# Second MLP: the square moves from layer one's outputs to layer two's loads, and the stretch of kept order moves with it

## The chip, the cores and the metric

One core of one Trainium2 chip runs the whole program. The metric is the time of the device in microseconds, the median of three runs. Smaller is better.

## The reference

Attention with a decay, then two MLPs over 2304 tokens of 512 features, each with a hidden layer of 2048. All in float32.

```python
scores = scale * q @ k.T + decay          # causal; softmax; times v -> x [2304, 512]
h = x @ w_in;   x = (h - tanh(h)) @ w_out            # first MLP
h = x @ w2_in;  r = maximum(h, 0); out = (r * r) @ w2_out   # second MLP
```

## The kernel before

**Arithmetic.** Matmuls take fp32r operands. Each float32 operand is split into a high part (a ScalarE copy into fp32r) and a low part (a VectorE subtraction), and a product is three matmuls, `PASSES`: high x high, high x low, low x high. "Split" below is always this pair, hi on ScalarE and lo on VectorE.

**Stages.** Attention first, with the first MLP threaded into it. The first MLP goes over blocks of 256 tokens, and its last block (`LAST`, 512 tokens) has 16 steps of 24 matmuls of 512 columns. In a step, `h1_atoms` makes 128 hidden features (L1010), then Tanh (L1020) on ScalarE, the difference (L1023) on VectorE, and the split (L1027, L1031) that the products of `y1_atoms` (L1050) of the next step read.

The second MLP uses a Strassen-like scheme: seven products of quarter blocks in place of eight, with sums of operands made beforehand and sums of results afterwards. In layer one, `l1_product` (L1220) computes for unit `u` (3 groups of tokens x 8 pairs of hidden chunks, 7 products of 384 columns each) products into shared PSUM banks. `after1` copies PSUM out on ScalarE (L1238), adds on VectorE (L1231), takes relu on ScalarE (L1234), and squares: on GpSimd in `store1` (L1265), or for one product in four on VectorE (L1261), which reads PSUM a second time. `put` stores the squares to `gscr` in DRAM.

In layer two there are 36 tiles `n` (9 blocks of 256 tokens x 4 chunks of the hidden features), each 42 matmuls of 256 columns (`l2_product`, L1382). For tile `n`, `g_load` brings four raw pieces by four DMAs on SP, `g_sums` makes four sums on VectorE with three instructions (L1334, L1335, L1337), and `g_split` splits seven operands of 256 (L1347 on ScalarE, 1792 elements a partition; L1348 on VectorE). `layer2` calls the sums and the split of tile `n + 2` and the load of tile `n + 4` while it issues tile `n`. There are four buffers for raw pieces and three for split ones. `after2` adds the results (L1395) and `store2` stores them. For the first tiles the same is called from layer one's list `events`, whose numbers count products: loads at 138, 145, 165, 170, sums at 146, 154, 171, and two special splits at 159 to 167.

**Weights.** The weights of the second MLP are loaded raw, decoded from their bits (`decode_w`: ScalarE L203 and L204, VectorE L210 and L212), combined to sums on GpSimd (`combine`, L256), and split piece by piece in `split_all` (L312, L313): first the two pieces of sums, then two raw pieces, `lag` calls apart. One decode at a time is under way; `decoded` starts the next. Weights of layer two go through `wscr` in DRAM and come back (`final_load`) to be split in `final_split`.

**Inputs of the second MLP.** `first_y_load` (step 6 of the last block) loads the first group, `y_sums` (step 8) makes four sums on GpSimd (L1176), and `y_split` splits seven pieces, one a step from step 9 on (L1164 on ScalarE, L1165 on VectorE).

**What sets the order.** Code is traced in the order of a clock (`cw`): each matmul atom is a tick, and `cw.later(k, fn)` traces `fn` k ticks on. The compiler's scheduler then orders each engine's instructions by its own estimate of when they are ready; every engine runs its list in that order. `pin` overrules it: while the list `ordered` isn't empty, the instruction is put behind whatever was traced last on its engine (`tc.keep_in_program_order`). `move` is a pinned DMA on SP. An instruction without `pin` can still move. Before, `ordered` is filled at unit 1 of layer one and stays filled to the end.

```python
def pin(ins):                       # L146
    if ordered:
        tc.keep_in_program_order(ins)
def store1(g, dst):                 # L1264
    nc.gpsimd.tensor_tensor(g, in0=g, in1=g, op=ALU.mult)
    cw.later(2, lambda: put(g, dst))
if n and x == 1 and n + 2 < NG:     # L1442, in layer2: x counts the products of tile n
    g_sums(n + 2)
if x == 3 and n + 2 < NG:
    g_split(n + 2)
    if n + 4 < NG:
        g_load(n + 4)
```

## Time and profile before

| | us |
|---|---|
| median of 3 runs | 1044.77 (1040.63 to 1045.24) |
| profiled execution | 1042.61 |
| its span | 1040.9 |
| TensorE busy | 1003.6 |
| VectorE, ScalarE, GpSimd busy | 721.4, 598.3, 412.1 |
| mean granted clock of TensorE, as a share of full speed | 0.986 |

In the rows below PE is TensorE, PEld its weight load, DVE VectorE, ACT ScalarE, POOL GpSimd, SP SyncE, whose queue (SPq) issues the DMAs. L12 is line 12 of the kernel. "a<-b" are the tiles written and read; a time in brackets is how long the engine sat idle before, and what released it. Matmul times are from issue to end and overlap, so the rate of matmuls is read from their count in a stretch. PEclk is the granted clock, 1.00 for 2.4 GHz and 0.50 for 1.2 GHz.

### The profile page before, as it was taken

To read this page: it belongs to the slowest core of one execution; us is meant where nothing else is said; L and a number is where in the kernel's file an instruction comes from. 1 tells how busy PE (TensorE), PEld (TensorE's weight loads), DVE (VectorE), ACT (ScalarE), POOL (GpSimd) and SP (SyncE) were. 2 spreads that over 40 slices of the span, in tenths; PEclk is the share of its full clock that TensorE was granted. 3 is DMA by queue.
4 is the path that set the end of the run, shared out by engine and by line. 5 is a ranking of instruction groups with operands and counts; after the bars stand their busy time and mean duration, and the time that the engine had idled before them with its cause. 6 is when DMAs were issued, how large, how long until landed. Compare 5 with 4: busy or idle time off the path is not lost. (4 is left out here: it accounts for less than half of the span.)

```text
span 1040.9 us, 20353 instructions
## 1 busy us (share of the span) xinstructions
PE 1003.6 (96%) x7134; PEld 953.5 (92%) x7134; DVE 721.4 (69%) x1521; ACT 598.3 (57%) x1245; POOL 412.1 (40%) x587
## 2 busy tenths in 40 slices
PE   7989999999999999999998999999999999999998
PEld 5778889999999999999997887999999898999998
DVE  4895963577677776777756578566566678777776
ACT  5895964566666666666644466557577564233332
POOL 3673542445554555544513234385756320000000
PEclk9998999999999999999998999999999999999999
DMA  8936653342343432442221232657868964344441
GB/s 233 284 109 216 207 149 74 81 121 72 90 125 95 102 105 77 122 110 67 65 66 41 95 122 81 206 204 250 269 232 263 330 203 128 102 132 133 122 122 41
DMA packets 188261, 146.97 MB, mean 141 GB/s; under 512 B 86688, under 2 KB 165856, under 8 KB 188160
## 3 DMA queue, kind: packets, MB, share of 16 engines
q1 hardware_dynamic: 188112, 145.65, 46.5%
q8 instruction: 56, 0.92, 0.4%
q14 instruction: 45, 0.37, 0.1%
q10 hardware_dynamic: 48, 0.03, 0.0%
HBM read 101.00 MB, written 39.92 MB: 135 GB/s over the span
## 5 line engine op out<-in xcount | busy, mean ns | idle before, releaser
L1050 PE MATMUL y<-ghl,w 128*128 128x256 f32 (+1 forms) x1536 | 246.7, 304 | 6.2 <-ACT ghl L1027 4.5
L1050 PEld LDWEIGHTS y<-ghl,w 128*128 128x128 f32 x1536 | 213.2, 193 | 19.5 <-ACT ghl L1027 4.9
L1010 PE MATMUL h<-x,w 128*128 128x256 f32 x1344 | 198.6, 289 | 6.4 <-POOL w L228 5.1
L1010 PEld LDWEIGHTS h<-x,w 128*128 128x128 f32 x1344 | 175.4, 191 | 11.3 <-POOL w L228 6.6
L1382 PE MATMUL o<-ws,gc 128*128 128x256 f32 x864 | 118.4, 283 | 0.0
L1347 ACT ACTIVATE gc<-graw 128x1792 fp32r<-128x1792 f32 x34 | 57.8, 1701 | 93.6 <-DVE graw L1337 52.4
L1220 PE MATMUL r<-yt,ws 128*128 128x384 f32 x576 | 107.0, 336 | 4.0 <-ACT g L1238 3.7
L1382 PEld LDWEIGHTS o<-ws,gc 128*128 128x128 f32 x864 | 110.1, 192 | 0.0
L1220 PEld LDWEIGHTS r<-yt,ws 128*128 128x128 f32 x576 | 99.9, 188 | 6.8 <-ACT g L1238 5.6
L1382 PE MATMUL o<-wq,gc 128*128 128x256 f32 x648 | 98.5, 287 | 6.2 <-DVE gc L1348 5.1
L1382 PEld LDWEIGHTS o<-wq,gc 128*128 128x128 f32 x648 | 85.8, 191 | 10.7 <-DVE gc L1348 9.3
L1265 POOL TENSOR_TENSOR g<-g 128x384 f32<-128x384 f32 x71 | 66.5, 945 | 71.2 <-ACT g L1234 52.4
L1348 DVE TENSOR_TENSOR gc<-graw,gc 128x1792 fp32r<-128x1792 f32 x34 | 68.8, 2024 | 35.3 <-ACT gc L1347 35.2
L680 ACT ACTIVATE Pb<-Pb,st 128x384 f32<-128x384 f32 (+2 forms) x80 | 55.3, 691 | 65.7 <-DVE st L671 65.4
L671 DVE CUSTOM_DVE_ANT_0 Pb<-s,Pb 128x128 f32<-128x128 f32 (+4 forms) x144 | 67.0, 481 | 29.1 <-PE s L743 23.2
L696 POOL TENSOR_SCALAR Pb<-Pb,st 128x384 f32<-128x384 f32 (+2 forms) x80 | 55.1, 689 | 77.2 <-DVE st L690 62.2
L1220 PE MATMUL r<-yt,wq 128*128 128x384 f32 x432 | 82.0, 340 | 1.4 <-DVE g L1261 1.4
L1220 PEld LDWEIGHTS r<-yt,wq 128*128 128x128 f32 x432 | 76.6, 191 | 2.8 <-DVE g L1261 2.3
L1023 DVE TENSOR_TENSOR g<-h,g 128x512 f32<-128x512 f32 x72 | 49.5, 688 | 29.1 <-ACT g L1020 27.7
L1231 DVE TENSOR_TENSOR g<-r,g 128x384 f32<-128x384 f32 x71 | 39.0, 552 | 32.2 <-ACT g L1238 17.4
L1234 ACT ACTIVATE g<-g 128x384 f32<-128x384 f32 x71 | 36.9, 522 | 42.2 <-DVE g L1231 41.8
L1020 ACT ACTIVATE g<-h 128x512 f32<-128x512 f32 x72 | 42.5, 590 | 31.4 <-PE h L1010 25.2
(169 smaller groups left out, 1929.8 us busy)
## 6 DMA issues: line engine op xcount, KB each, us to landing
graw<-gscr SPq DMA_DIRECT2D x144, 128.0 KB, 2.6
gscr<-g SPq DMA_DIRECT2D x95, 192.0 KB, 3.3
wraw<-in_moe_w_in_dram SPq DMA_DIRECT2D x32, 512.0 KB, 4.5
wraw<-in_moe_w_out_dram SPq DMA_DIRECT2D x32, 512.0 KB, 5.5
neg<-cscr SPq DMA_DIRECT2D x32, 288.0 KB, 3.3
qk<-in_k_dram SPq DMA_DIRECT2D x48, 128.0 KB, 2.8
v<-in_v_dram SPq DMA_DIRECT2D x48, 128.0 KB, 2.7
K<-K SPq DMA_DIRECT2D x32, 144.0 KB, 2.4
```

The lines of the kernel that those rows point to most:

```text
L671: nc.vector.tensor_tensor_reduce(out=d, in0=t[:rows, src : src + m], in1=d, scale=-0.125, scalar=3.0e38 if j == 0 else stat(0, x)[:rows], ...
L680: nc.scalar.activation(d, d, AF.Exp, bias=stat(len(parts) - 1, x)[:rows], scale=-1.0, accum_out=stat(2, x)[:rows])
L696: nc.gpsimd.tensor_scalar(d, d, r, 1.0, op0=ALU.mult, op1=ALU.mult)
L1010: nc.tensor.matmul(o, lhsT=win(fc, wh, dc), rhs=xpart(j, dc, xh), start=dc == 0 and wh + xh == 0, stop=dc == ND - 1 and wh == 1)
L1020: nc.scalar.activation(g, t, AF.Tanh)
L1023: nc.vector.tensor_tensor(g, t, g, op=ALU.subtract)
L1050: nc.tensor.matmul(o, lhsT=wout(fc, wh, i * P, P), rhs=ghl[:, xh, fj * n : fj * n + n], start=s == 0 and fj == 0 and wh + xh == 0 and i % ...
L1220: nc.tensor.matmul(t, lhsT=wprod(1, p, k, wh)[:, dc * P : (dc + 1) * P], rhs=yt[i, k][:, xh, dc], start=k in FRESH and dc == 0 and wh + xh ...
L1265: nc.gpsimd.tensor_tensor(g, in0=g, in1=g, op=ALU.mult)
L1347: pin(nc.scalar.activation(hi, t[:, 1:8], AF.Copy))
L1348: pin(nc.vector.tensor_tensor(lo, in0=t[:, 1:8], in1=hi.bitcast(F32), op=ALU.subtract))
L1382: nc.tensor.matmul(o, lhsT=gc[n][gh, e][:, GWHERE[k]] if n == 1 else gc[n][gh][:, GWHERE[k], e], rhs=wprod(2, 2 * q + e, k, wh), start=q = ...
```

## The change

The outputs of layer one are stored after relu, without the square: `store1` and VectorE's L1261 go, and all four results of a unit are stored two ticks after their relu. Layer two squares a tile's four raw pieces in one ScalarE instruction (128x1024) at the head of `g_sums`; the pieces and sums change places in the tile, so that the raw pieces lie side by side, and `GWHERE` follows. The three sums keep their shapes.

`ordered` is filled at step 0 of the first MLP's last block and emptied at tile 4 of layer two. Tanh, the difference and the split of the first MLP and the splits of the first group of inputs (`y_split` with `i == 0`) are pinned now, as far as `ordered` holds. In `split_all` the raw pieces of a weight come before the sums, and the delays become 1, 2 and 1 ticks.

```diff
--- before.py
+++ after.py
@@ -271,7 +271,7 @@
         v = full.rearrange("p (c f) -> p c f", c=ND)
         s4 = sums.rearrange("p (k f) -> p k f", k=4)
         work = split_plan(1, p, (v[:, :, 0:P], v[:, 2:4, P : 2 * P]), [s4[:, 0:2], s4[:, 2:4]])
-        split_all(1, p, work, 1)
+        split_all(1, p, work[2:] + work[:2], (1, 2, 1))
 
     wscr = [dram.tile([P, 7, 256], F32, name=f"wscr_{p}") for p in range(NP2)]
 
@@ -314,7 +314,7 @@
             if phase == 2:
                 pin(low)
             if x + 1 < len(work):
-                cw.later(lag, lambda: one(x + 1))
+                cw.later(lag[x], lambda: one(x + 1))
             else:
                 ready_w.add((phase, p))
                 if phase == 1:
@@ -346,7 +346,7 @@
 
     def final_split(p):
         *s_, r = stagew.pop(p)
-        split_all(2, p, split_plan(2, p, (r[:, 1:3], r[:, 0:1]), s_), 1)
+        split_all(2, p, split_plan(2, p, (r[:, 1:3], r[:, 0:1]), s_), (1, 1, 1))
 
     WHERE = {1: {5: 0, 6: 1, 7: 2, 3: 3, 1: 4, 2: 5, 4: 6}, 2: {5: 0, 6: 1, 7: 2, 4: 3, 2: 4, 3: 5, 1: 6}}
 
@@ -1017,18 +1017,18 @@
             g = m1.tile([P, 512], F32, tag="g", name=f"g1_{j}_{s}", bufs=3)
             ghl = m1.tile([P, 2, 512], F32R, tag="ghl", name=f"ghl1_{j}_{s}", bufs=2)
             gt[j, s] = ghl
-            nc.scalar.activation(g, t, AF.Tanh)
+            pin(nc.scalar.activation(g, t, AF.Tanh))
 
             def sub():
-                nc.vector.tensor_tensor(g, t, g, op=ALU.subtract)
+                pin(nc.vector.tensor_tensor(g, t, g, op=ALU.subtract))
                 cw.later(LAG['hi'], hi)
 
             def hi():
-                nc.scalar.activation(ghl[:, 0], g, AF.Copy)
+                pin(nc.scalar.activation(ghl[:, 0], g, AF.Copy))
                 cw.later(LAG['lo'], lo)
 
             def lo():
-                nc.vector.tensor_tensor(ghl[:, 1], g, ghl[:, 0].bitcast(F32), op=ALU.subtract)
+                pin(nc.vector.tensor_tensor(ghl[:, 1], g, ghl[:, 0].bitcast(F32), op=ALU.subtract))
             cw.later(LAG['sub'], sub)
 
         return [(6 * n, lambda i=i: a(i)) for i in range(len(todo))]
@@ -1070,6 +1070,8 @@
         raw = {}
         for i, (j, s) in enumerate(steps):
             last = j == LAST
+            if last and s == 0:
+                yield 0, (lambda: ordered.append(True)), j
             if s == 6 and j == LAST - 1:
                 yield 0, (lambda: raw.__setitem__(LAST, x_last())), j
             if s == 7 and j < LAST - 1:
@@ -1161,8 +1163,8 @@
 
     def y_split(i, k, src):
         t = y_tile(i, k)
-        nc.scalar.activation(t[:, 0], src, AF.Copy)
-        nc.vector.tensor_tensor(t[:, 1], src, t[:, 0].bitcast(F32), op=ALU.subtract)
+        (pin if i == 0 else lambda ins: ins)(nc.scalar.activation(t[:, 0], src, AF.Copy))
+        (pin if i == 0 else lambda ins: ins)(nc.vector.tensor_tensor(t[:, 1], src, t[:, 0].bitcast(F32), op=ALU.subtract))
 
     def y_load(i, raws_):
 
@@ -1240,7 +1242,7 @@
         def finish(g, b, r, c):
             add(g, b, g)
             relu(g, g)
-            cw.later(1, lambda: store1(g, gscr[i][:, 2 * p + r, c]))
+            cw.later(2, lambda: put(g, gscr[i][:, 2 * p + r, c]))
 
         if k == 1:
             hold(m1.tile([P, NU1], F32, tag="x", name=f"g00_{u}", bufs=4))
@@ -1258,12 +1260,7 @@
         elif k == 4:
             g = m1.tile([P, NU1], F32, tag="x", name=f"g10_{u}", bufs=4)
             relu(g, t)
-            nc.vector.scalar_tensor_tensor(g, in0=t, scalar=0.0, in1=g, op0=ALU.max, op1=ALU.mult)
-            cw.later(1, lambda: put(g, gscr[i][:, 2 * p + 1, 0]))
-
-    def store1(g, dst):
-        nc.gpsimd.tensor_tensor(g, in0=g, in1=g, op=ALU.mult)
-        cw.later(2, lambda: put(g, dst))
+            cw.later(2, lambda: put(g, gscr[i][:, 2 * p + 1, 0]))
 
     def put(g, dst):
         move(dst, g.rearrange("p (b n) -> p b n", b=3))
@@ -1273,8 +1270,6 @@
         for s in range(n):
             if s == 0:
                 load_w(2, 0)
-            if s == 1:
-                ordered.append(True)
             if s < NP2:
                 feed.upto(NF + s + 1)
             for pos, (d, k) in enumerate(STEP):
@@ -1308,7 +1303,7 @@
             events.setdefault(at, []).append((fn, arg))
     AT2 = {1: (0, 0), 6: (0, 256), 7: (1, 0), 2: (1, 256), 5: (2, 0), 4: (2, 256), 3: (3, 0)}
     ORDER2 = (1, 6, 7, 2, 5, 4, 3)
-    GWHERE = {7: 0, 5: 1, 6: 2, 3: 3, 1: 4, 2: 5, 4: 6}
+    GWHERE = {7: 3, 5: 4, 6: 5, 3: 6, 1: 0, 2: 1, 4: 2}
     graws, gc, r2 = {}, {}, {}
     NG = NBLK * 4
 
@@ -1323,18 +1318,21 @@
     def g_load(n):
         j, q = divmod(n, 4)
         t = graws[n] if n in graws else g_tile(n)
-        for slot, h, i in ((0, 1, 0), (5, 0, 0), (7, 1, 1), (6, 0, 1)):
+        for slot, h, i in ((0, 1, 0), (1, 0, 0), (3, 1, 1), (2, 0, 1)):
             src = gscr[j // 3][:, 4 * q : 4 * q + 4, h, j % 3].rearrange("p (e i) t -> p i e t", i=2)
             move(t[:, slot], src[:, i])
 
     def g_sums(n):
         t = graws[n]
-        x = t[:, 7]
-        both = bass.AP(tensor=x.tensor, offset=x.offset, ap=[x.ap[0], [0, 2], [1, 2 * P]])
-        pin(nc.vector.tensor_tensor(t[:, 1], in0=t[:, 0], in1=t[:, 5], op=ALU.subtract))
-        pin(nc.vector.tensor_tensor(t[:, 2:4].rearrange("p k e t -> p k (e t)"),
-                                    in0=t[:, 0:2].rearrange("p k e t -> p k (e t)"), in1=both, op=ALU.add))
-        pin(nc.vector.tensor_tensor(t[:, 4], in0=t[:, 6], in1=t[:, 3], op=ALU.subtract))
+        raw = t[:, 0:4].rearrange("p k e t -> p (k e t)")
+        pin(nc.scalar.activation(raw, raw, AF.Square))
+
+        def two(x, step):
+            return bass.AP(tensor=x.tensor, offset=x.offset, ap=[x.ap[0], [step * 2 * P, 2], [1, 2 * P]])
+
+        pin(nc.vector.tensor_tensor(t[:, 4], in0=t[:, 0], in1=t[:, 1], op=ALU.subtract))
+        pin(nc.vector.tensor_tensor(two(t[:, 5], 1), in0=two(t[:, 0], 4), in1=two(t[:, 3], 0), op=ALU.add))
+        pin(nc.vector.tensor_tensor(t[:, 7], in0=t[:, 2], in1=t[:, 6], op=ALU.subtract))
 
     def gc_tile(n):
         t = box2["m3"].tile([P, 2, 7, 2, P], F32R, tag=f"gc{n % 3}", name=f"gc_{n}", bufs=1)
@@ -1433,6 +1431,8 @@
     def layer2():
         third()
         for n in range(NG):
+            if n == 4:
+                ordered.clear()
             for x, k in enumerate(ORDER2):
                 if n == 0 and x < 3:
                     continue
```

## Rows read from the trace of the kernel before

**Rows 1.** the page's first part: busy time, share of the span and instructions of each engine.
```profile
PE 1003.6 (96%) x7134; PEld 953.5 (92%) x7134; DVE 721.4 (69%) x1521; ACT 598.3 (57%) x1245; POOL 412.1 (40%) x587
```

**Rows 2.** busy time by stretch: length, busy us (instructions) by engine, PEclk, DMA share, GB/s.
```profile
575.00:650.00 75.00, 73.59 (x324) 60.33 (x323) 54.09 (x80) 44.59 (x81) 24.92 (x28) 1.00 0.29 99
...
850.00:875.00 25.00, 22.37 (x178) 21.35 (x177) 22.14 (x30) 12.20 (x12) 0.26 (x1) 1.00 0.56 172
875.00:900.00 25.00, 25.00 (x210) 25.00 (x210) 17.81 (x27) 8.27 (x6) 0.00 (x0) 1.00 0.47 133
900.00:1025.00 125.00, 121.54 (x979) 118.21 (x978) 94.13 (x135) 42.83 (x30) 0.00 (x0) 1.00 0.40 116
```

**Rows 3.** TensorE's waits, 560 to 1041 us: total, times, longest.
```profile
PE y L1050 <- ACT ghl L1027: 4.5, 1, 4.5
PE r L1220 <- ACT g L1238: 3.7, 4, 2.1
...
PE r L1220 <- DVE g L1261: 1.4, 3, 0.8
...
PE o L1382 <- DVE gc L1348: 5.1, 10, 0.8
```

**Rows 4.** timeline, 545 to 580 us: start, length, instruction, [idle before <-releaser].
```profile
550.14 9.46 DVE L1165 TENSOR_TENSOR yt<-yr,yt 128x768 fp32r<-128x768 f32 x4 [1.67 <-ACT yt L1164]
...
559.52 0.68 DVE L1023 TENSOR_TENSOR g<-h,g 128x512 f32<-128x512 f32 x1
...
560.91 0.58 PE L1050 MATMUL y<-ghl,w 128*128 128x256 f32 x1 [4.48 <-ACT ghl L1027]
```

**Rows 5.** busy time by stretch, behind the two longest waits (columns as in 2).
```profile
560.90:565.20 4.30, 4.06 (x17) 3.77 (x18) 3.02 (x5) 2.17 (x3) 0.00 (x0) 0.50 0.01 4
...
824.60:828.00 3.40, 3.20 (x10) 3.20 (x11) 2.20 (x5) 1.77 (x4) 0.83 (x1) 0.50 0.92 315
```

**Rows 6.** timeline, 790 to 862 us.
```profile
819.76 1.06 ACT L312 ACTIVATE ws<-wst 128x1024 fp32r<-128x1024 f32 x1 [3.29 <-DMA wst<-wscr]
...
823.27 1.33 PE L1220 MATMUL r<-yt,ws 128*128 128x384 f32 x6 [2.13 <-ACT g L1238]
```

**Rows 7.** groups, 850 to 1041 us: shapes xcount | busy, mean ns | idle before <-releasers.
```profile
L1348 DVE TENSOR_TENSOR gc<-graw,gc 128x1792 fp32r<-128x1792 f32 x34 | 68.8, 2024 | 35.3 <-ACT gc L1347 35.2
L1347 ACT ACTIVATE gc<-graw 128x1792 fp32r<-128x1792 f32 x34 | 57.8, 1701 | 93.6 <-DVE graw L1337 52.4 <-issue 27.1 <-DMA graw<-gscr 11.6
```

**Rows 8.** timeline of VectorE, 848 to 1041 us.
```profile
914.17 0.42 DVE L1334 TENSOR_TENSOR graw<-graw 128x256 f32<-128x256 f32 x1
...
919.61 0.42 DVE L1334 TENSOR_TENSOR graw<-graw 128x256 f32<-128x256 f32 x1
...
955.64 0.69 DVE L1335 TENSOR_TENSOR graw<-graw 128x512 f32<-128x512 f32 x1
956.25 2.02 DVE L1348 TENSOR_TENSOR gc<-graw,gc 128x1792 fp32r<-128x1792 f32 x1
```

**Rows 9.** groups of the input splits (L1164 whole span, L1165 655 to 850 us).
```profile
L1164 ACT ACTIVATE yt<-yr 128x768 fp32r<-128x768 f32 x19 | 15.9, 842 | 8.5 <-POOL yr L1176 3.3 <-PE r L1220 2.3 <-DMA yr<-yscr 1.5
...
L1165 DVE TENSOR_TENSOR yt<-yr,yt 128x768 fp32r<-128x768 f32 x12 | 12.9, 1079 | 3.1 <-ACT yt L1164 3.0
```

**Rows 10.** timeline, 622 to 634 us.
```profile
630.91 2.79 PE L1050 MATMUL y<-ghl,w 128*128 128x512 f32 x11 [1.41 <-DVE ghl L1031]
```

**Rows 11.** groups, and SP's waits, both 655 to 850 us.
```profile
L1265 POOL TENSOR_TENSOR g<-g 128x384 f32<-128x384 f32 x71 | 66.5, 945 | 71.2 <-ACT g L1234 52.4 <-DVE wfull L212 7.5 <-issue 6.1
...
L1261 DVE SCALAR_TENSOR_TENSOR g<-r,g 128x384 f32<-128x384 f32 x24 | 13.2, 551 | 10.6 <-ACT g L1234 10.6
...
SPq L151 <- POOL g L1265: 65.2, 34, 8.7
```

**Rows 12.** groups of ScalarE, whole span.
```profile
L312 ACT ACTIVATE ws<-wst 128x1024 fp32r<-128x1024 f32 x5 | 5.3, 1056 | 3.5 <-DMA wst<-wscr 3.5
...
L428 ACT ACT_TABLE_LOAD x1 | 1.3, 1283 | 0.0
```


## The prediction

> **What bounds the kernel now.** The page's first part comes first: TensorE is busy for 96% of the span [rows 1]. So only what still stops TensorE, or slows it, can be gained, and the question is where the missing microseconds lie. The busy time by stage tells that. From 875 to 900 us, in the second MLP's layer two, TensorE issued 210 matmuls of 256 columns without a gap, 119 ns each; from 900 to 1025 us it issued 979, which at 119 ns are 116.5 us, so 8.5 us of these 125 were lost; from 850 to 875 us it issued 178, or 21.2 us, so 3.8 were lost [rows 2]. TensorE's own waits name the rest: one wait of 4.5 us in the first MLP's last part, 3.7 us for ScalarE's copies out of PSUM (L1238) and 1.4 us for VectorE's L1261 in layer one, 5.1 us for VectorE's L1348 in layer two [rows 3]. Three places, three mechanisms.
>
> *First MLP, at its last block.* The timeline [rows 4] shows four of VectorE's L1165 (splits of the second MLP's input, traced much later) in one stretch from 550.14 that lasts 9.46 us, because each needs a sum that GpSimd has just begun. L1023, which the running block needs, stands behind them until 559.52, and TensorE waits 4.48 us. In the 4.3 us after that, the granted clock is 0.50, the level of 1.2 GHz instead of 2.4 [rows 5]: half of 4.3, 2.15 us more. Together 6.6 us.
>
> *Layer one.* ScalarE sat 3.29 us at L312 until a DMA of staged weights landed, its copies came late, and TensorE waited 2.13 us [rows 6]; then 3.4 us ran at a clock of 0.50 [rows 5], 1.7 us more: 3.8 us.
>
> *Layer two.* VectorE goes round a closed chain: sums, then a wait for ScalarE's split (L1347, 1.70 us), then its own split (L1348, 2.02 us), then the next sums. From the sums at 914.17 to those at 919.61 that is 5.44 us [rows 7, 8], while a tile's 42 matmuls take 42 x 0.119 = 5.0 us. VectorE isn't full: 94.1 us of work in 23.3 tiles (979/42), 4.0 us each [rows 2]. Its order makes the period. Where the order was broken once, L1348 started at 956.25 straight behind the next tile's sums, with no wait in its row [rows 8].
>
> **The change, part by part.** The sum stands against the profiled execution, 1042.6 us (span 1040.9), 2.2 us under the median of the runs.
>
> *Order kept from the last block on.* Tanh, both splits behind it, the input splits, their loads on SP and the decoding of weights now stay in traced order, so the L1165 that blocked at 550 us can't stand there. Gain: 6.6 at most, nothing at least (if L1023 finds another blocker). I take 6.6, since every instruction that stood ahead of L1023 is one that is moved.
>
> What is moved has to go somewhere. Seven ScalarE splits of 0.84 us (5.9) and seven of VectorE of 1.08 (7.6) [rows 9], traced one a step, now fall into steps 9 to 15 of the block. A step is 24 matmuls; 324 took 75 us, so 5.56 us a step, 39 us for seven. VectorE was busy 54.1 of 75 us there, 72%, and gets 19% more: 91%. ScalarE goes from 59% to 75% [rows 2]. Behind a late VectorE stand L1023 and L1031, and TensorE behind these; one such wait is already there, 1.41 us [rows 10]. Bounds: nothing, or one such wait in each of the seven steps, 9.9 us. I take two, 2.8 us, as 91% leaves room on the mean but not at each moment. The twelve input loads on SP now start at step 6 and GpSimd's four sums at step 8; DMA was busy 0.29 and GpSimd 33% [rows 2], and ScalarE's next use of them is at steps 9 to 15: I cost them at nothing. Without that cover, ScalarE would stop at a pinned split with Tanh queued behind it.
>
> *Raw weights split before their sums, with delays 1, 2, 1.* No work is added; a decode ends about one atom later (5.56/6, 0.9 us), and GpSimd gets that time for the sums. Cost nothing, hidden by the steps between a decode and its first product; without them 0.9 us at layer one's start.
>
> *Layer one without squares.* 71 of GpSimd's L1265 (945 ns) and 24 of VectorE's L1261 (551 ns) go [rows 11]. GpSimd's time is off TensorE's path, VectorE's isn't: the 1.4 us of waits [rows 3] go, since PSUM is free once ScalarE's relu has read it. The stores waited 65.2 us on SP for the squares [rows 11]; now they go sooner, and the loads of weights queued behind them too. Whether that brings forward the load behind the 3.8 us is open: that load can be late from traffic alone. Between nothing and 3.8, I take the middle, 1.9.
>
> *Squares in layer two.* One on ScalarE for each of 36 tiles, 128x1024. No row shows a Square; the nearest is a ScalarE copy of the same shape, 1.056 us [rows 12]. ScalarE had 42.8 us of work in 23.3 tiles, 1.84 each [rows 2]; 2.9 of 5.0 fits beside the rest. If Square needs a table not loaded, one load is 1.283 us [rows 12]; below nothing there is none, as no work goes. Three squares fall in layer one's tail ahead of copies that TensorE needs: nothing to 3 x 1.06 us; I take 0.5, since a copy has about two products of slack.
>
> *Order freed from tile 4 on.* The next sums can run while ScalarE splits, and VectorE's 4.0 us fit into 5.0. Bounds: nothing (the compiler keeps the same order) and 8.5 us, of which I take 7, a little being left to stores and adds that now move as well. The 3.8 us before 875 us stay: those tiles keep their order. SP's loads are freed too; they are ahead by four buffers.
>
> Sum: 6.6 - 2.8 + 1.4 + 1.9 - 0.5 + 7.0 = 13.6 us; 1042.6 - 13.6 = **1029**.
>
> **Rivals.**
> *A, the last block gives its gain back.* VectorE at 91% makes a wait in each step: 9.9 instead of 2.8 us, 1036. For it: the block already shows one such wait while VectorE was less busy. Against it: the ordered layer one has only waits of this size, few of them.
> *B, freeing changes no order.* No 7 us: 1036. Against it: the one place where the order did break.
> *C, nothing new comes, and what is left goes too:* 6.6 + 1.4 + 3.8 + 8.5, 20.3 us, 1022; with the 1.41 us and part of the 3.8 before 875 us, down to 1018.
> *D, slower: the square enters the chain.* If a tile's data land only when VectorE's split of the tile before has ended, ScalarE's square, and all ScalarE work behind it, waits: the period is 5.44 + 1.06 = 6.5 us against 125/23.3 = 5.4 now, 1.1 us in each of 32 tiles, 36 us; less the 6.6 of the last block, 1072. It decides from the point where the loads run less than a tile ahead. Against it: loads wait on buffers freed four tiles earlier.
> The Trainium skill (ScalarE: Activation LUTs, Rules for kernel authors) speaks against the change here: multiplications belong on VectorE rather than ScalarE. By that rule the square would be a worse choice on ScalarE; D is how that would show, and no run here shows either. An estimate from L1348's 2.02 us for 1792 elements puts it at 1.2 us on VectorE, whose 4.0 us would become 5.2 of 5.0, so I expect the trace to go against the rule.
> *E, it doesn't do what it says:* the order in the last block binds nothing and the rest is small, 1041 to 1043.
>
> **How the numbers follow.** Forecast 42%, A 18, B 10, C 17, D 8, E 5. A measurement can tell about 0.5%, 5.2 us, from no change: faster means under 1039.5, slower over 1050. Faster: the forecast's 40, C 17, two thirds of A and B 19, and 2 of E's edge: 0.78. Slower: D, and 2 for A at twice its price: 0.10. The rest, 0.12, is the same. The range takes in C below, with 2 us for the small waits, 1016, and A, B and E above, 1042; D and the tails are left out.
>
> **What would show it.** Right: no L1165 ahead of 590 us, no TensorE gap and no 0.50 clock near 560; no wait for L1261; VectorE's sums of a tile starting before L1348 of the tile before it, and about 210 matmuls in every 25 us of layer two. Wrong: a chain period of 6 us or more there with ScalarE waiting for loads (D), an unchanged 5.4 (B), or waits of TensorE for L1027 or L1031 between 610 and 655 us that add up to over 6 us (A).

## The result, and the profile after

| | before | after |
|---|---|---|
| median of 4 runs each, us | 1043.61 (1040.63 to 1045.24) | 1027.84 (1026.06 to 1029.55) |
| ratio, 95% interval | | 0.9852 (0.982 to 0.9884) |
| profiled execution, us | 1042.61 | 1026.77 |
| its span, us | 1040.9 | 1025.1 |

The changed kernel is 1.5% faster, and its median lies 1.2 us from the forecast of 1029. That says nothing yet of the terms of the sum, so the traces are compared stage by stage. In the changed kernel the lines have moved by a little: the input splits L1164 and L1165 are now L1166 and L1167, GpSimd's sums L1176 are L1178, the copies L1238 are L1240, the squares stand at L1328, VectorE's sums L1334 to L1337 at L1333 to L1335, and the splits L1347 and L1348 at L1345 and L1346.

The page's first part, of the changed kernel [before: rows 1]:

```profile
PE 997.0 (97%) x7134; PEld 950.9 (93%) x7134; DVE 702.0 (68%) x1497; ACT 631.8 (62%) x1281; POOL 348.4 (34%) x515
```

GpSimd has lost 64 us of work and VectorE 19, ScalarE has gained 34. TensorE has as many matmuls as before, so again only its gaps can have shrunk. TensorE's waits over the whole span (total, times, longest; those for the second MLP and the last block of the first):

```profile
PE y L1050 <- DVE ghl L1031: 4.6, 3, 3.7
...
PE o L1380 <- DVE gc L1346: 2.5, 3, 0.8
...
PE r L1222 <- ACT g L1240: 0.7, 3, 0.4
```

Against [rows 3]: the wait for the copies in layer one went from 3.7 to 0.7 us, the one for VectorE's L1261 is gone with L1261, the one for VectorE's split in layer two went from 5.1 to 2.5. In the last block the 4.5 us for L1027 are gone, and 4.6 us for VectorE's L1031 have come in their place. The busy time by stretch of the changed kernel (length, then PE, PEld, DVE, ACT and POOL busy with their instructions, clock, DMA share, GB/s):

```profile
540.00:575.00 35.00, 35.00 (x243) 32.73 (x242) 11.76 (x18) 10.62 (x18) 0.00 (x0) 1.00 0.20 65
...
609.60:613.00 3.40, 3.40 (x8) 2.72 (x9) 3.33 (x6) 0.89 (x2) 0.74 (x1) 0.51 0.02 5
850.00:875.00 25.00, 21.83 (x175) 21.01 (x175) 23.91 (x35) 16.35 (x15) 0.00 (x0) 1.00 0.47 135
875.00:900.00 25.00, 25.00 (x211) 25.00 (x210) 20.83 (x32) 15.56 (x14) 0.00 (x0) 1.00 0.46 135
900.00:1009.00 109.00, 109.00 (x911) 109.00 (x910) 85.81 (x121) 59.66 (x46) 0.00 (x0) 1.00 0.41 121
```

The old gap near 560 us has vanished, but there are now 3.4 us at a granted clock of half (1.2 GHz) behind the new wait, from 609.6 us on. From 875 us on TensorE runs without a gap: 911 matmuls in 109 us are 119.6 ns each, the pace that [rows 2] showed only for 875 to 900 us. The stretch from 850 to 875 us still lacks some 34 matmuls of that pace (25 us at 119.6 ns are 209), as it lacked 31 before.

To put one number on each stage, take for every matmul the time until the next one starts, subtract its columns at 2.4 GHz and 13.3 ns, and add up what is left. The 13.3 ns are fitted to the changed kernel's trace: from 575 us on, half of its matmuls of 256, 384 and 512 columns start within 120, 173 and 227 ns of the one before, and the formula gives 120.0, 173.3 and 226.6. Half clock counts in it as well as gaps do. **TensorE's lost time** by stretch, us, in all the kernels of this study (one profiled execution each):

| kernel | to 540 | last block, 540 to 660 | layer one, 660 to 842 | first tiles of layer two, 842 to 875 | from 875 |
|---|---|---|---|---|---|
| before | 89.5 | 9.0 | 10.5 | 3.9 | 8.1 |
| after | 89.5 | 7.5 | 3.6 | 4.2 | 0.04 |
| e1_order_to_end | 89.8 | 8.5 | 4.4 | 3.7 | 15.8 |
| e2_order_from_unit1 | 92.2 | 8.9 | 3.3 | 4.2 | 0.04 |
| e3_gpsimd_squares_back | 91.0 | 7.5 | 9.3 | 4.7 | 0.04 |
| e4_second_psum_read_back | 90.6 | 7.4 | 3.1 | 4.5 | 0.04 |
| e5_sums_one_a_step | 92.4 | 5.6 | 3.2 | 4.2 | 0.04 |
| e6_sums_on_vector | 91.9 | 5.7 | 4.2 | 4.2 | 0.04 |
| e8_square_on_vector | 87.7 | 7.6 | 4.4 | 16.7 | 1.1 |
| e9_sums_first | 85.0 | 11.7 | 3.9 | 5.2 | 0.04 |
| e10_order_unit1_sums_vector | 94.1 | 2.7 | 2.7 | 4.2 | 0.04 |
| e11_e10_free_from_tile2 | 93.2 | 2.6 | 2.5 | 5.6 | 0.04 |
| e12_e10_free_from_tile0 | 92.1 | 2.5 | 4.2 | 5.7 | 0.04 |
| e13_before_freed | 89.8 | 10.1 | 8.9 | 7.8 | 1.1 |

From before to after this gives 1.5 us in the last block, 6.9 in layer one, -0.3 in the first tiles and 8.1 from 875 us on, together 16.2; the spans differ by 15.8, since the end behind the last matmul has become 0.5 longer. The first 540 us, which no edit touches, scatter by up to 9 us from execution to execution. So differences of a few us between whole times are read from the stretch that the edit touches. Such a stretch scatters too, by less: the last block lies between 7.4 and 8.5 in the five kernels that have it as the changed kernel does (after, e1, e3, e4, e8), layer one between 2.5 and 4.4 in the ten that have it without squares. A difference of 1 us or so shows nothing by itself. In e8 and e13 the first tiles end only after 875 us, and their 1.1 in the last column still belongs to them: counted by matmul instead of by time, the first tiles lose 17.8 and 8.9 us there, and the rest 0.04.

### The profile page after: what moved, and what is told of

It reads as the page before. It is cut to its first block, busy times and chain, and to the rows that moved or that the text cites. A ratio compares the mean times of both kernels' runs of the same rounds, so it can differ in the third digit from the quotient of the medians.

```text
span 1025.1 us, 20205 instructions
## 1 busy us (share of the span) xinstructions
PE 997.0 (97%) x7134; PEld 950.9 (93%) x7134; DVE 702.0 (68%) x1497; ACT 631.8 (62%) x1281; POOL 348.4 (34%) x515
## 4 chain that ended last, share of the span: by engine, by line
PE 81%; DVE 5%; ACT 4%; issue 3%; DMA 3%; POOL 2%; SPq 1%; DVEq 0%; ACTq 0%; POOLq 0%
PE y L1050 17%; PE h L1010 17%; PE o L1380 15%; PE r L1222 13%; PE pv L860 3%; PE pt L777 3%; PE s L742 2%; PE s L743 2%; PE pv L822 2%; PE s L711 2%; PE pt L761 1%; POOL w L228 1%; DVE wq L313 1%; DMA graw<-gscr 1%; DMA gscr<-g 1%
## 5 line engine op out<-in xcount | busy, mean ns | idle before, releaser
L1380 PE MATMUL o<-ws,gc 128*128 128x256 f32 x864 | 116.4, 283 | 0.0
L1380 PEld LDWEIGHTS o<-ws,gc 128*128 128x128 f32 x864 | 109.3, 192 | 0.0
L1380 PE MATMUL o<-wq,gc 128*128 128x256 f32 x648 | 91.5, 284 | 3.2 <-DVE gc L1346 2.5
L256 POOL TENSOR_TENSOR wsum<-wfull 128x256 f32<-128x256 f32 x32 | 31.5, 985 | 164.7 <-DVE wfull L212 136.3
L1380 PEld LDWEIGHTS o<-wq,gc 128*128 128x128 f32 x648 | 83.7, 192 | 4.0 <-DVE gc L1346 3.2
L1346 DVE TENSOR_TENSOR gc<-graw,gc 128x1792 fp32r<-128x1792 f32 x34 | 68.6, 2022 | 24.2 <-ACT gc L1345 24.1
L1345 ACT ACTIVATE gc<-graw 128x1792 fp32r<-128x1792 f32 x34 | 57.7, 1699 | 33.2 <-PE o L1380 22.9
L1023 DVE TENSOR_TENSOR g<-h,g 128x512 f32<-128x512 f32 x72 | 49.4, 687 | 38.2 <-ACT g L1020 36.7
L1027 ACT ACTIVATE ghl<-g 128x512 fp32r<-128x512 f32 x72 | 45.2, 628 | 35.1 <-DVE g L1023 34.5
```

Source lines behind the costliest of these rows:

```text
L1023: pin(nc.vector.tensor_tensor(g, t, g, op=ALU.subtract))
L1027: pin(nc.scalar.activation(ghl[:, 0], g, AF.Copy))
L1345: pin(nc.scalar.activation(hi, t[:, 1:8], AF.Copy))
L1346: pin(nc.vector.tensor_tensor(lo, in0=t[:, 1:8], in1=hi.bitcast(F32), op=ALU.subtract))
L1380: nc.tensor.matmul(o, lhsT=gc[n][gh, e][:, GWHERE[k]] if n == 1 else gc[n][gh][:, GWHERE[k], e], rhs=wprod(2, 2 * q + e, k, wh), start=q = ...
```

## The experiments

Each edit is made in the changed kernel, unless it says otherwise. The times are medians of timed runs, beside 13 runs of the kernel before on the same chip (their median was 1041.32 for e1 to e4, 1041.43 for e5, e6, e8 and e10, 1042.65 for e9 and e11 to e13).

### Layer two: is it the freed order?

**The order kept to the end.**

```
-            if n == 4:
-                ordered.clear()
```

> The changed kernel with one part undone: order is kept to the end of layer two. Theory (the chain of VectorE's sums, ScalarE's split, VectorE's split sets the period): the sums come round every 5.44 us again, TensorE waits at tile after tile for VectorE, about 8 us more than the changed kernel, 1034 to 1037; the square, a ScalarE instruction that fits beside VectorE's split, adds nothing to the 5.44. Rival (the square enters the chain): a period of about 6.5 us, some 36 us more, over 1060. Rival (the order is the same without the pins): under 2 us more.

1044.7 us, ratio 1.0026 (1.0004 to 1.0048): the whole gain is gone, which is more than the theory gave (1034 to 1037). VectorE's timeline with the order kept (start, length, instruction, idle before), and then ScalarE's:

```profile
933.23 0.42 DVE L1333 TENSOR_TENSOR graw<-graw 128x256 f32<-128x256 f32 x1
...
936.68 2.02 DVE L1346 TENSOR_TENSOR gc<-graw,gc 128x1792 fp32r<-128x1792 f32 x1 [1.85 <-ACT gc L1345]
938.62 0.42 DVE L1333 TENSOR_TENSOR graw<-graw 128x256 f32<-128x256 f32 x1
```

```profile
934.95 1.70 ACT L1345 ACTIVATE gc<-graw 128x1792 fp32r<-128x1792 f32 x1 [2.74 <-DVE graw L1335]
936.55 1.04 ACT L1328 ACTIVATE graw<-graw 128x1024 f32<-128x1024 f32 x1
```

This is the chain of [rows 8], here with a period of 5.4 us: sums, a wait of 1.85 us for ScalarE's split, VectorE's split, the next sums. In the changed kernel the same stage looks like this:

```profile
904.39 0.41 DVE L1333 TENSOR_TENSOR graw<-graw 128x256 f32<-128x256 f32 x1
...
906.46 2.03 DVE L1346 TENSOR_TENSOR gc<-graw,gc 128x1792 fp32r<-128x1792 f32 x1 [0.46 <-ACT gc L1345]
909.11 0.42 DVE L1333 TENSOR_TENSOR graw<-graw 128x256 f32<-128x256 f32 x1 [0.63 <-ACT graw L1328]
...
911.50 2.03 DVE L1346 TENSOR_TENSOR gc<-graw,gc 128x1792 fp32r<-128x1792 f32 x1 [0.78 <-ACT gc L1345]
```

```profile
902.91 1.06 ACT L1328 ACTIVATE graw<-graw 128x1024 f32<-128x1024 f32 x1 [1.50 <-DMA graw<-gscr]
904.72 1.70 ACT L1345 ACTIVATE gc<-graw 128x1792 fp32r<-128x1792 f32 x1 [0.75 <-PE o L1380]
908.02 1.06 ACT L1328 ACTIVATE graw<-graw 128x1024 f32<-128x1024 f32 x1 [1.60 <-DMA graw<-gscr]
```

Here ScalarE's split of 904.72 runs while VectorE adds up the next tile (904.39 to 906.0), and the period, 906.46 to 911.50, is 5.04 us, a tile's matmuls. ScalarE's split waits for TensorE to give a buffer back (L1380), so TensorE sets the pace. What I had not foreseen is the size of the loss with the order kept, 15.8 us where the kernel before loses 8.1. The two traces tell where it comes from. In the kernel before, the order breaks at five places from 875 us on, as in the last two of [rows 8]: two sums of the next tile run ahead of a split, and the next split follows after 4.25 us. Everywhere else the splits follow each other after 5.43 to 5.94 us. With the order kept and the square there, it breaks nowhere, and all periods are 5.39 to 5.80 us, 5.58 on average. So the square doesn't lengthen the chain; what is lost is the breaks. Why they are lost I read so: with the square pinned on ScalarE behind the split of the tile before, VectorE has nothing to run ahead with. That reading was not tried by itself; that freeing is worth 15.8 us once the square is there is shown.

**The kernel before, with the order freed and nothing else.**

```
+            if n == 4:
+                ordered.clear()
```

> The kernel before with one part of the change alone: order freed from tile 4 of layer two on; squares stay in layer one. Theory (freeing is what gains in layer two, with or without the square): the 8 us lost after 875 us go, 1033 to 1036, and the waits before 875 us stay. Rival (freeing pays only for the square, which would have cost more under kept order): under 3 us.

1039.26 us, ratio 0.9967 (0.995 to 0.9985), between the theory's 1033 to 1036 and the rival's. Behind the first tiles the 8.1 us of loss go to 0.04: freeing alone removes all of it, without the square. But the first tiles lose 8.9 us (counted by matmul) instead of 3.9. VectorE there, then TensorE:

```profile
858.73 0.43 DVE L1334 TENSOR_TENSOR graw<-graw 128x256 f32<-128x256 f32 x1 [2.49 <-DMA graw<-gscr]
859.19 0.43 DVE L1337 TENSOR_TENSOR graw<-graw 128x256 f32<-128x256 f32 x1
```

```profile
861.53 0.80 PE L1382 MATMUL o<-wq,gc 128*128 128x256 f32 x2 [3.25 <-ACT gc L1347]
```

A freed sum of a later tile (L1334) was placed ahead of the last sum (L1337) of the tile that TensorE needed. It waited 2.49 us for its own load, L1337 stood behind it on the queue, and TensorE stopped for 3.25 us. A freed instruction can be moved back as well as forward.

**The square on VectorE instead of ScalarE.**

```
-        pin(nc.scalar.activation(raw, raw, AF.Square))
+        pin(nc.vector.tensor_tensor(raw, in0=raw, in1=raw, op=ALU.mult))
```

> The changed kernel with layer two's square on VectorE, as one multiplication of 128x1024, instead of ScalarE. Theory (VectorE's work of 4.0 us a tile becomes about 5.2, over TensorE's 5.0): VectorE sets the period in layer two, 0.2 to 0.6 us a tile over 36 tiles, 6 to 20 us more than the changed kernel. Rival (the skill's page, ScalarE: Activation LUTs, Rules for kernel authors: a multiplication belongs on VectorE): no slower, ScalarE's wait for it gone, within 2 us or faster.

1040.52 us, ratio 0.9998 (0.9981 to 1.0015): the gain is lost, by an amount inside the 6 to 20 us that I gave, but that is luck, since the loss is not where I had put it. The steady part runs at full pace, with VectorE 95% busy (118.62 of 125 us):

```profile
900.00:1025.00 125.00, 125.00 (x1044) 125.00 (x1043) 118.62 (x161) 43.73 (x30) 0.00 (x0) 1.00 0.41 119
```

A square takes 1.22 us there and VectorE's tile some 4.8 of 5.0 us, not the 5.2 that I had estimated. The loss is 16.7 us in the first tiles. It begins at one place on VectorE's timeline, and this is what TensorE makes of it:

```profile
851.09 1.23 DVE L1328 TENSOR_TENSOR graw<-graw 128x1024 f32<-128x1024 f32 x1 [2.14 <-DMA graw<-gscr]
852.24 0.42 DVE L1335 TENSOR_TENSOR graw<-graw 128x256 f32<-128x256 f32 x1
```

```profile
854.56 0.80 PE L1380 MATMUL o<-wq,gc 128*128 128x256 f32 x2 [5.39 <-ACT gc L1345]
```

Again a freed instruction of a later tile, here the square, waits for its load ahead of the sum that the running tile needs. TensorE stops for 5.39 us, then again for 3.42 us before 866.31 and 1.88 us before 869.41, and runs at a mean granted clock of 0.73 from 850 to 875 us. The first of these stops is rival D's mechanism (a square that waits for data, with the chain behind it), on another engine and at one place instead of 32.

### Layer one: what did the squares cost?

**GpSimd's squares back in layer one** (the features are then squared twice).

```
-            cw.later(2, lambda: put(g, gscr[i][:, 2 * p + r, c]))
+            cw.later(1, lambda: store1(g, gscr[i][:, 2 * p + r, c]))
...
+    def store1(g, dst):
+        nc.gpsimd.tensor_tensor(g, in0=g, in1=g, op=ALU.mult)
+        cw.later(2, lambda: put(g, dst))
```

> The changed kernel with GpSimd's three multiplications a unit put back into layer one (layer two squares as well, so these features come out to the fourth power). Theory (the squares hold up the stores on SP, and with them the loads of weights that ScalarE waits for): SP waits for GpSimd some 60 us in layer one, ScalarE's L312 waits 2 us or more for a DMA near 815 us, TensorE stops there, 3 to 6 us more than the changed kernel. Rival (that wait is the traffic's, and went by chance of another order): SP waits, but TensorE loses less than 1 us.

1034.08 us, ratio 0.9922 (0.9891 to 0.9953). Layer one loses 9.3 instead of 3.6 us: the squares on GpSimd cost 5.7. The load that I had named (L312, near 815 us) accounts for only 1.3 us of loss; the cost is spread out, and TensorE's waits for L1240 alone are 4.1 us in seven waits. The longest of them in the timeline of this kernel, SP, ScalarE, TensorE:

```profile
738.26 1.58 SPq L151 DMA_DIRECT2D wscr<-wfull  x2
...
746.36 0.66 ACT L203 ACTIVATE wfull<-wraw 128x512 uint32<-128x512 uint32 x1 [2.22 <-DMA wscr<-wsum]
...
747.47 0.48 ACT L1240 ACTIVATE g<-r 128x384 f32<-128x384 f32 x1
...
748.01 1.31 PE L1222 MATMUL r<-yt,ws 128*128 128x384 f32 x6 [1.32 <-ACT g L1240]
```

In the changed kernel the same two stores leave here:

```profile
733.56 0.94 SPq L151 DMA_DIRECT2D wscr<-wfull  x2
```

The decode L203 writes `wfull`, so it needs the two stores of `wfull` to have ended. They landed 7.1 and 6.5 us after their issue, at 745.33 and 745.98, just before it started (the store of `wsum` that the row names landed only at 748.3). It waited 2.22 us on ScalarE, the copy L1240 stood behind it, and TensorE waited 1.32 us for the copy. In the changed kernel the same decode waits 1.30 us.

That the stores left later because of the squares isn't shown here. The two leave after 5053 and 5060 matmuls of the program, in the changed kernel after 5055 and 5058: at the same point of the work, and what grew is the time to landing (5.8 and 6.0 us there). At the decode of 694.52, which waits 2.10 us, the stores did leave later, after 4783 and 4787 matmuls instead of 4776 and 4780, some 1.2 us. SP's waits in the two kernels have nearly the same total (for GpSimd's squares 73.2 us, for ScalarE's relu 71.0), so the total of a queue's waits told nothing here.

There is another way in which the squares can cost, which I did not test: they run beside VectorE's work, and its instructions with two inputs in SBUF get longer (what that is, the last block shows below). From 660 to 838 us the nine L210 that write `wraw` take 1073 ns on average with the squares and 799 without, the twelve L1167 from `yr` 1133 and 1026. So it is shown that the squares cost 5.7 us, and how they do it stays open in part.

**L1261's product back on VectorE**, only that, with the store one tick behind it (the same features are again squared twice).

```
+            nc.vector.scalar_tensor_tensor(g, in0=t, scalar=0.0, in1=g, op0=ALU.max, op1=ALU.mult)
```

> The changed kernel with VectorE's second read of PSUM (the product of relu with the PSUM bank, one in four results) put back into layer one; these features come out to the fourth power. Theory: TensorE waits again for that instruction at a few places, 1 to 2.5 us in total more than the changed kernel, at most 1 of it anywhere. Rival (VectorE has room and the bank is free in time): no wait for it, less than 0.5 us.

1027.82 us, ratio 0.986 (0.983 to 0.989), layer one 3.1 us, and TensorE waits for VectorE nowhere in it. L1261 cost nothing by itself. The 1.4 us of waits for it in [rows 3] were, as I read it, waits for a VectorE that was late for other reasons; which ones was not tried.

### The last block: what made the old wait, and the new one?

**The order kept from unit 1 of the second MLP on, not from the last block on.**

```
-            if last and s == 0:
-                yield 0, (lambda: ordered.append(True)), j
...
+            if s == 1:
+                ordered.append(True)
```

> The changed kernel with one part undone: order is kept from unit 1 of layer one on, as before, not from the first MLP's last block. Theory (both places lose to the same thing, GpSimd's four sums running while VectorE must work, and the order only moved them from 550 to 601 us): the wait near 556 us comes back, 4 to 5 us and a stretch at half clock, the one near 606 us goes, and the time is within 3 us of the changed kernel. Rival (keeping the order there removed 6.6 us for good): 5 to 8 us slower.

1029.62 us, ratio 0.987 (0.9844 to 0.9897). The old wait comes back and the new one goes. VectorE, then TensorE's waits from 545 to 665 us:

```profile
552.45 9.48 DVE L1165 TENSOR_TENSOR yt<-yr,yt 128x768 fp32r<-128x768 f32 x4 [1.40 <-ACT yt L1164]
...
561.86 0.68 DVE L1023 TENSOR_TENSOR g<-h,g 128x512 f32<-128x512 f32 x1
```

```profile
PE y L1050 <- ACT ghl L1027: 4.1, 1, 4.1
PE y L1050 <- DVE ghl L1031: 1.6, 2, 1.1
```

8.9 us are lost in the block instead of 7.5, little more than the scatter of this stretch. The order here moved a loss from 560 to 606 us and hardly shrank it. The changed kernel at the new place:

```profile
601.14 7.86 POOL L1178 TENSOR_TENSOR yr<-yr,yr 128x768 f32<-128x768 f32 x4
601.24 2.03 DVE L313 TENSOR_TENSOR wq<-wfull,wq 128x256 fp32r<-128x256 f32 x1 [1.47 <-ACT wq L312]
...
603.19 0.68 DVE L1023 TENSOR_TENSOR g<-h,g 128x512 f32<-128x512 f32 x1
...
605.09 2.24 DVE L313 TENSOR_TENSOR ws<-wsum,ws 128x512 fp32r<-128x512 f32 x1 [1.22 <-ACT ws L312]
...
607.25 2.30 DVE L1031 TENSOR_TENSOR ghl<-g,ghl 128x512 fp32r<-128x512 f32 x1
...
609.60 4.33 PE L1050 MATMUL y<-ghl,w 128*128 128x512 f32 x11 [3.67 <-DVE ghl L1031]
```

While GpSimd runs its four sums, VectorE's splits, which read two tiles in SBUF, take 2.0 to 2.3 us. Just before them the same L313 on 128x512 and the same L1031 took 0.69 and 0.68 us (592.60 and 593.21), and L313 on 128x256 takes 0.43 where nothing runs beside it (e6, below). L1023 reads one of its two inputs from PSUM and takes its usual 0.68 us in the middle of it. So the four L1165 that [rows 4] shows at 9.46 us did not take that long by waiting for their data: 1.93 to 2.55 us each, they were splits of 0.95 us that ran beside sums on GpSimd. In the kernel before, L1023's own input comes from this Tanh:

```profile
555.29 0.58 ACT L1020 ACTIVATE g<-h 128x512 f32<-128x512 f32 x1
```

It is there at 555.87, 3.65 us before L1023 starts at 559.52. The two L1165 that VectorE still runs in that time begin at 554.68 and 557.04 and take 2.44 and 2.55 us; at 0.95 us each they would have ended 3.1 us sooner. The rest of the 3.65 us is the order, and the sums' share in it: ScalarE's L1164 ahead of the later splits did wait for them, 1.67 us at most.

**One sum to a step instead of all four together.**

```
-            cw.later(2 * x, lambda x=x: y_sum(i, x))
+            cw.later(6 * x, lambda x=x: y_sum(i, x))
```

> The changed kernel with GpSimd's four input sums traced one a step (6 ticks apart) instead of two ticks apart. Theory (while GpSimd runs a sum, a VectorE instruction with two operands in SBUF stands until it ends, and four sums in a row are more than the slack): each sum still stretches one VectorE instruction to about 2 us, but TensorE's wait of 3.7 us near 606 us and the 3.4 us at half clock go, 3 to 5 us less than the changed kernel, 1022 to 1025. Rival (VectorE is simply full there, at 91%): the wait stays, within 1.5 us of the changed kernel.

1027.51 us, ratio 0.9868 (0.9847 to 0.989). The wait of 3.7 us and the half clock behind it are gone; in their place stand five waits of 3.9 us together, 1.6 at most. The block loses 5.6 us instead of 7.5. So the wait went as the theory said, but the gain is 1.9 us there and not 3 to 5, and the whole time does not differ from the changed kernel's.

**The four sums on VectorE.**

```
-        pin(nc.gpsimd.tensor_tensor(r[o], in0=r[a], in1=r[b], op=ALU.subtract))
+        pin((nc.gpsimd if i else nc.vector).tensor_tensor(r[o], in0=r[a], in1=r[b], op=ALU.subtract))
```

> The changed kernel with the first group's four input sums on VectorE instead of GpSimd: 3.8 us more work on VectorE. Theory (contention): no VectorE instruction of two SBUF operands is over 1.3 us between 600 and 612 us, the 3.7 us wait goes or falls under 1.5 us, no half clock, 3 to 5 us less than the changed kernel. Rival (VectorE is full there): the added work makes the wait longer, 2 to 4 us slower than the changed kernel.

1025.15 us, ratio 0.9847 (0.9819 to 0.9874); the block loses 5.7 us. VectorE, from 600 to 612 us:

```profile
603.73 0.43 DVE L313 TENSOR_TENSOR wq<-wfull,wq 128x256 fp32r<-128x256 f32 x1 [1.46 <-ACT wq L312]
...
607.79 0.95 DVE L1178 TENSOR_TENSOR yr<-yr,yr 128x768 f32<-128x768 f32 x1
```

A sum takes 0.95 us on VectorE (1.49 beside GpSimd's L256), half of what it took on GpSimd, and nothing is stretched to over 1.2 us before 612 us. Half of the expected gain is there; the rest sits in five waits of 2.9 us together, of a VectorE that has more to do in these steps. The whole time does not differ from the changed kernel's here either.

**Both: order from unit 1 on, and sums on VectorE** (the edits of e2 and e6).

> Order kept from unit 1 on, as before the change, and the four input sums on VectorE. VectorE's list near 550 us still has the input splits (L1165) ahead of the block's L1023, and four sums more. Theory (contention made the old wait too): the L1165 take 0.95 us instead of 2.4, and the wait of TensorE near 558 us falls from 4.1 us to under 1; 4 to 7 us less than with the sums on GpSimd in this order (1029.6), 1023 to 1026. Rival (the old wait came from the order, L1023 standing behind the splits): the wait stays at 3 us or more.

1022.72 us, ratio 0.9818 (0.9783 to 0.9853), the block loses 2.7 us. L1023 again has four instructions of the input ahead of it on VectorE, now one L1165 and three sums, and nothing holds VectorE up:

```profile
554.66 0.95 DVE L1165 TENSOR_TENSOR yt<-yr,yt 128x768 fp32r<-128x768 f32 x1
...
555.52 1.82 DVE L1176 TENSOR_TENSOR yr<-yr,yr 128x768 f32<-128x768 f32 x2
...
557.26 0.68 DVE L1023 TENSOR_TENSOR g<-h,g 128x512 f32<-128x512 f32 x1
...
558.73 0.95 DVE L1165 TENSOR_TENSOR yt<-yr,yt 128x768 fp32r<-128x768 f32 x1
559.60 0.68 DVE L1031 TENSOR_TENSOR ghl<-g,ghl 128x512 fp32r<-128x512 f32 x1
```

```profile
540.00:575.00 35.00, 35.00 (x260) 33.47 (x259) 21.28 (x31) 15.84 (x25) 0.00 (x0) 1.00 0.28 84
600.00:625.00 25.00, 24.93 (x110) 20.34 (x110) 18.56 (x29) 16.01 (x29) 8.53 (x9) 1.00 0.31 106
```

No gap near 560 us, none at 606. This edit alone does not part the two causes, since the list is not the old one (three of the four L1165 come after L1023 now) and the sums are done sooner on VectorE. Together with the lengths of the bars above, it says that most of the old wait was GpSimd running beside VectorE, and the smaller part the order. This kernel has the lowest ratio of the study: 4.8 us less lost in the block than in the changed kernel. Its ratio and the changed kernel's overlap at the ends of their intervals, so the gain over the changed kernel is shown in the stretches, and not yet in the whole times.

**The sums split before the raw weights again**, as before the change.

```
-        split_all(1, p, work[2:] + work[:2], (1, 2, 1))
+        split_all(1, p, work, (1, 1, 1))
```

> The changed kernel with the old order of a weight's pieces put back: sums before raw pieces, one tick apart. Theory (raw pieces first only give GpSimd time for the sums): ScalarE waits some us more for GpSimd's L256 at L312 in the last block, and TensorE's waits there grow by 0 to 3 us. Rival (the part is needed now that ScalarE's list is kept in order, since Tanh stands behind a split that waits for GpSimd): 4 us or more slower.

1033.03 us, ratio 0.9904 (0.9875 to 0.9933). The block loses 11.7 us instead of 7.5. All engines' waits of this kernel from 570 to 660 us:

```profile
ACT ws L312 <- POOL wsum L256: 17.2, 7, 3.2
...
PE y L1050 <- DVE ghl L1031: 7.0, 5, 4.3
```

ScalarE stands for 17.2 us at splits whose sums GpSimd has not finished, and with the order kept everything of the running block queues behind them. This is what the rival said. The new order of the splits, with its delays, which I had costed at nothing, is worth 4.2 us here.

### What is left in the first tiles

**e10, freed two tiles earlier, and freed from the first tile on.**

```
-            if n == 4:
+            if n == 2:
```

> The best kernel so far (order from unit 1 on, input sums on VectorE, 1022.7) with order freed from tile 2 instead of tile 4 of layer two. Theory (the four waits of 0.6 to 1.0 us that are left at the start of layer two come from tiles 2 to 5, whose sums and splits are still in kept order): 1 to 3 us less, 1020 to 1022. Rival (VectorE is short of time there with the last weights to split, whatever the order): within 1 us.

> The same with order freed from tile 0. Theory as for tile 2: 1 to 4 us less than 1022.7. Rival (the last weights' splits now run ahead of the first tiles' splits on VectorE, and TensorE waits for tile 2): 2 us or more slower.

The second has `if n == 0:`. 1024.33 us, ratio 0.9825 (0.9803 to 0.9847), and 1026.32 us, ratio 0.9847 (0.982 to 0.9873). The first tiles lose 5.6 and 5.7 us instead of 4.2. The small waits for VectorE's split shrink from 2.5 to 0.8 us, as the theory had it, but one longer wait for ScalarE's comes instead (TensorE's waits of the kernel freed from tile 2, from 842 us on, then ScalarE and VectorE):

```profile
PE o L1380 <- ACT gc L1345: 2.7, 1, 2.7
PE o L1380 <- DVE gc L1346: 0.8, 1, 0.8
```

```profile
846.34 1.06 ACT L1328 ACTIVATE graw<-graw 128x1024 f32<-128x1024 f32 x1 [2.45 <-DMA graw<-gscr]
...
847.43 0.42 DVE L1333 TENSOR_TENSOR graw<-graw 128x256 f32<-128x256 f32 x1 [2.14 <-DMA graw<-gscr]
847.77 0.42 DVE L1335 TENSOR_TENSOR graw<-graw 128x256 f32<-128x256 f32 x1
```

It is the pattern of e13 and e8 once more: the square of a later tile waits 2.45 us for its load, that tile's freed sum waits with it on VectorE, and L1335, which the running tile's split needs, stands behind the sum. From 852.90 us on 3.4 us run at a granted clock of 0.50 besides. So part of these tiles' 4 us does come from the kept order (the 1.7 us of small waits that went), but freeing it this early brings back more than it takes away.

## Why the prediction was right, and where its steps were not

The sum was 13.6 us, and the spans differ by 15.8. Two terms were too small, one was too large, and one part that I had put at nothing made the change work. That the sum came out so near is in part luck: the last block's 2.3 us too much stand against layer one's 4.1 too little.

- **Layer two, 7.0 forecast, 7.8 measured** (8.1 from 875 us on, less 0.3 in the first tiles). The mechanism is the one I gave: the next tile's sums run during ScalarE's split, and the period falls from 5.4 to 5.0 us (e1; e13 shows that freeing alone does it). That the tiles ahead of 875 us keep their loss was right as well.
- **The square at nothing: right, with a condition that I did not state.** It takes 1.06 us and ScalarE waits for TensorE besides. But with the order kept, the same square makes the stage lose 15.8 us instead of 8.1 (e1). The two edits are not two terms; the second is what makes the first free.
- **Layer one, 1.4 + 1.9 - 0.5 = 2.8 forecast, 6.9 measured.** I had priced the squares by the waits that the view named, and took half of 3.8 us for the store queue. GpSimd's squares alone cost 5.7 us (e3), in many small delays whose way to TensorE is shown only in part. Of the 3.8 us at L312, most comes and goes from one execution to another: e13 has the same layer one as the kernel before, and there L312 waits 1.53 us instead of 3.29 and TensorE 0.38 instead of 2.13. L1261, to which I gave 1.4, cost nothing by itself (e4). Nothing is left to show the 0.5 us for squares in the tail: TensorE's waits for L1240 are 0.7 us in all.
- **Last block, 6.6 - 2.8 = 3.8 forecast, 1.5 measured**, little more than the scatter of this stretch. This is the step that failed, and rival A is half true. I wrote that each L1165 took long "because each needs a sum that GpSimd has just begun". The runs show that VectorE's instructions with two SBUF inputs are held up while GpSimd runs (e2, e5, e6); waiting for the sums had only the smaller part. So keeping the order did take the L1165 away from L1023, but GpSimd's four sums, moved to step 8, now hold up L313 and L1031 there; I had costed these sums at nothing. It was not the 91% of VectorE that made the wait of 3.7 us: with 3.8 us more work on VectorE (e6) it is gone. The smaller waits that remain in e5 and e6, 3.9 and 2.9 us, may be VectorE's load; that was not tried.
- **The order of the weight splits, costed at nothing**, is worth 4.2 us (e9). Without it the kept order would have made the last block slower than before, 11.7 against 9.0 us.
- **The rivals.** B (freeing changes nothing) is out by e1, E by the result. A's sign, over 6 us of waits in the last block, did not come: they are 4.6 in the whole block. C asked for the last block's gain to come whole, and it did not. D did not come in the changed kernel: of the 28.3 us that ScalarE's squares waited for loads from 850 us on, in 23 waits, none ended as a wait of TensorE after 875 us. Its mechanism is real, though, and shows in the first tiles of e8 and e11; e13 has it with a sum in place of the square.

On the rule of the Trainium skill (ScalarE: Activation LUTs, Rules for kernel authors) that multiplications belong on VectorE: on these shapes in float32 the square takes 1.22 us on VectorE and 1.06 us on ScalarE, and the kernel with the square on VectorE comes out at a ratio to before of 0.9998 against 0.9852. So the measurement speaks against the rule here, but because of the order on VectorE's queue, not because of VectorE's load, as I had argued. The reason that the Trainium skill gives there is a speed in bf16, which no run here shows.

## What to carry to other kernels

When an instruction takes two or three times its usual time, look at what runs beside it before looking for what it waits for: a bar that is too long and has no idle time before it points to a shared resource, and reordering such work only moves the loss to the next neighbour. An order pinned by hand pays until a wait inside it closes a chain; free it there, but see that no freed instruction whose load is not there yet lands ahead of one that is needed now. Work on an engine that nobody seems to wait for can still cost: TensorE's waits in layer one never name GpSimd, and the squares there cost 5.7 us. Put such work back alone and measure it, before you price it from the list of waits.

## What the runs showed of the hardware

VectorE and GpSimd hold each other up. In the changed kernel, beside GpSimd's sums, VectorE's subtraction on 128x512 with both inputs in SBUF took 2.24 and 2.30 us instead of 0.69, on 128x256 2.03 instead of 0.43. With one input in PSUM it took 0.68 us in the same stretch. GpSimd is held up too: its four sums took 7.86 us beside these, and 9.40 us beside the four L1165 of e2, where four of 1.85 us, as L1178 takes in layer one of e3, would be 7.4. The three VectorE instructions ended 0.3 to 0.6 us after the sum beside them. The Trainium skill states this (SBUF — State Buffer, SBUF: two separate sides): the two engines share a pair of SBUF ports that one instruction locks for its whole length, and a VectorE instruction needs it when it has two SBUF inputs and GpSimd reads SBUF. The trace agrees, in the lengths, in where the instructions end and in the exception of L1023.

TensorE's clock: after the gap of 3.67 us before 609.60 the granted clock was half for 3.4 us, at a cost of some 1.7 us on top of the wait. With the same work spread so that no wait was longer than 1.6 us (e5), there was none of it in that block.
